# Second batch's transposed q and k in two single PSUM banks instead of the halves of a double tile, with a new order of all operations

## Chip, cores, metric

The kernel runs on one core of one Trainium2 chip. The metric is device time in microseconds (us) of one execution, as the median of several runs; lower is better.

## What is computed

Attention with a few extra "beacon" keys, and then a two-layer network with an ELU between the layers:

```
q, k, v: [B=8, H=8, S=576, D=64];  beacon_k, beacon_v: [8, 8, 16, 64]
k_all, v_all = beacon first, then k, v               # 592 keys per head
scores = q @ k_all.T / 8, causal over the 576 keys, beacons always seen
a = softmax(scores);  x = (a @ v_all) as [B*S = 4608, H*D = 512]
h = x @ w_in                                         # w_in  [512, 2048]
g = h where h > 0, else exp(h) - 1
out = g @ w_out                                      # w_out [2048, 512], float32
```

## The kernel before

Everything is cut into small steps, and the order in which they are issued is one long list of words in the code. Each engine carries out its own steps in the order of the list; semaphores, which the framework derives from the data, join the engines. A word is `step.batch.pair.part`, and a word `lv.0.1:bk` has a gate after the colon: this DMA may be issued only when the step `bk` is done. Heads are worked on in four pairs per batch.

The steps that the rest of the text names, by engine:

- POOL issues the loads. `lq.b.i.h0.h1` loads q (i = 0) or k (i = 1) of batch b for heads h0 to h1 into SBUF; only batches 0 and 1 use it. `ld` converts a quarter of a later batch's q or k into a DRAM copy. `lv`, `lb` load v, `wi` and `wo` the weights. `id` and `tri` make the identity and the triangular mask.
- SP issues `ct.b.p`: for batches 2 to 7, two DMA transposes (q and k of a pair) from the DRAM copy into the transposed tile `qk`. It also issues `s`, the stores of the output.
- PE: `T.b.p.i` transposes q or k of pair p, twelve small transposes into PSUM (batches 0 and 1). `bt` transposes the beacons' keys. `S` computes scores, `L` and `W` (batches 0) or `Y` and `Z` (later) the sums of the softmax and the products with v. `F.t.i` is a part of the first layer for token tile t, `G.t.b.q` a quarter of a 128-token block of the second. `warm.n.rows.bank.k` issues n matmuls on zeros whose results nobody reads.
- ACT: `x` is the exponential of scores, `n` and `N` the reciprocal of the sums (a logarithm, then an exponential), `e` the exponential of the ELU.
- DVE: `m` masks, `a` adds exponentials up, `M` and `V` scale the attention's output into `xT`, `r` and `g` finish the ELU, `cb` copies beacon keys into `qk`, `bs` and `bk` prepare them.
- ACT or DVE, by the last letter of the word: `cp.b.p.i` copies what T left in PSUM into `qk` (bfloat16), and `o` copies a finished block of the output out of PSUM. The last block, `os.9.3`, is copied in two halves.

Tiles of tokens: the first 512 tokens are two tiles of 256 (t = 0, 1), the others have 512 (t = 2 to 9). Batch 0 is computed in two halves of its queries (`A`, 256 queries, and `B`), so that the first tile's F can start early: `L.0.A`, `n.0.A`, `W.0.A` and `M.0.A` come ahead of it.

PSUM has eight banks here. Four of them are handed out singly by `bank()`, and T of batch 0, `bt`, `W`, `L.0.A`, `F`, `G` and the warm matmuls use them. The other four make two double tiles, handed out by `pair()`: S, L.0.B, Y and Z use them, and T of batch 1, where q and k of one pair are the two halves of one double tile. Which of the banks a step gets is written in the strings of `slots`, read one digit at each allocation. A step that gets a bank waits until the last reader of its former content is done.

Of the kernel before, what the change touches and what calls it, by code (L numbers as in the profile page):

```python
# [10 lines left out]
BF16 = mybir.dt.bfloat16  # L11
# [6 lines left out]
def kernel(  # L18
# [14 lines left out]
    B, H, S, D = q.shape  # L33
# [23 lines left out]
            "082746153804275613804275618302475613"),  # L57
        "bank": (
            "03213201320132013210213210320123010203123012021023013231023012301213210323310232"
            "30213021023023132032103212312013020213201303203213230103120310321323201321013031"  # L60
            "203102101203120312321201230130213220"),
        "qk": (
            "07651432065714320657142306574132"),
        "S": (
            "01010101010101010101010101010010101001010110010101001100101010100110011010011010"
            "010101001011001011011001101001011001101001101010101001011010"),
# [185 lines left out]
    @step  # L252
    def T(b, p, i):
        if b == 0:
            dst = tps[b, p, i] = bank(BF16, "tqk")
        else:
            if (b, p) not in tps:
                tps[b, p] = pair("tp", BF16)
            dst = tps[b, p, i] = tps[b, p][:, i, :]
        for r in range(R):  # L260
            for h in range(2):
                nc.tensor.transpose(
                    out=dst[D * h:D * (h + 1), PR * r:PR * (r + 1)],
                    in_=st[b, i][:, 2 * p + h, r, :],
                    identity=identb[0:PR, 0:PR],
                )
# [315 lines left out]
    warm.11.128.bank.0 lq.0.0.0.2 lq.0.1.0.2 lq.0.1.4.8 lq.0.0.4.8 lq.0.1.2.4 id lq.0.0.2.4 bs  # L582
    T.0.0.1 bt T.0.0.0 bk warm.4.64.bank.1 cp.0.0.0.A cp.0.0.1.V cb.0.0 lq.1.0.0.4:cp.0.0.0.A
    S.0.0.2 T.0.3.1 x.0.0.2 S.0.0.3 tri cp.0.3.1.V T.0.2.1 x.0.0.3 S.0.0.0 cp.0.2.1.V
    lq.1.1.0.4:cp.0.0.1.V T.0.3.0 x.0.0.0 S.0.0.1 lv.0.1:bk cp.0.3.0.V T.0.2.0 x.0.0.1
    warm.1.64.bank.1 cb.0.1 cp.0.2.0.V S.0.3.3 T.0.1.1 x.0.3.3 cb.0.2 S.0.2.2 cb.0.3 cp.0.1.1.V
    lb.0:cb.0.2 T.0.1.0 x.0.2.2 S.0.2.0 lv.0.2:cb.0.2 cb.1.0 warm.1.64.bank.0 cp.0.1.0.V x.0.2.0
    S.0.3.0 warm.2.64.bank.0 cb.1.1 m.0.0.3 lv.0.0:cp.0.2.0.V x.0.3.0 S.0.1.0 m.0.2.0
    warm.2.64.bank.0 wi.1.0:cb.0.0 cb.1.2 m.0.0.0 x.0.1.0 S.0.3.2 warm.2.128.bank.0 m.0.3.0 x.0.3.2
    m.0.3.3 T.1.0.1 T.1.0.0 cb.1.3 m.0.1.0 wi.1.1:m.0.3.3 cp.1.0.1.A S.0.2.3 cp.1.0.0.V L.0.A  # L590
    x.0.2.3 lv.0.4:cb.1.2 T.1.1.0 n.0.A wi.0.1:cp.0.2.0.V S.0.1.3 cp.1.1.0.V T.1.1.1
    warm.4.64.bank.0 wi.0.0:cp.1.0.0.V cp.1.1.1.V x.0.1.3 wi.2.0:cb.1.1 S.0.1.2 W.0.A.1 m.0.1.3
    wi.2.1:cp.1.0.0.V x.0.1.2 S.0.2.1 M.0.A.1 lv.0.3:m.0.0.0 W.0.A.0 x.0.2.1 m.0.0.2 S.1.0 M.0.A.0
    lq.1.1.4.8:cp.1.1.1.V x.1.0.0 S.1.2 F.0.3 lq.1.0.4.8:m.0.3.0 x.1.2.0 wi.3.0:cp.0.1.0.V S.0.1.1
    F.0.2 x.0.1.1 e.0.3 S.0.3.1 S.1.4 x.0.3.1 F.0.1 r.0.3 m.0.2.2 m.0.2.3 x.1.4.1 wi.3.1:m.0.2.2
    m.0.3.2 F.0.0 g.0.3 wo.0:m.0.2.3 e.0.2 m.0.1.2 S.1.5 e.0.0 L.0.B r.0.2 lb.1:g.0.3 m.1.2.0 e.0.1
    g.0.2 x.1.5.1 F.0.5 r.0.1 r.0.0 n.0.B g.0.0 S.1.1 lv.1.4:r.0.0 W.0.B.1.1 g.0.1 lv.1.2:g.0.0
    W.0.B.0.1 e.0.5 M.0.B.1.1 x.1.1.0 T.1.2.1 r.0.5 ld.2.0.144:g.0.1 F.0.4 M.0.B.0.1 m.1.4.1 m.1.5.1
    T.1.3.1 wo.1:m.1.4.1 cp.1.2.1.V T.1.3.0 cp.1.3.1.A T.1.2.0 g.0.5 W.0.B.0.0 cp.1.2.0.A cp.1.3.0.V
    W.0.B.1.0 m.1.1.0 S.1.3 M.0.B.0.0 S.1.9 lv.1.0:cp.1.3.0.V x.1.3.0 M.0.B.1.0 F.0.7 e.0.4 m.1.3.0  # L600
    x.1.3.1 r.0.4 F.0.6 m.1.0.0 g.0.4 e.0.7 lv.1.1:m.1.0.0 m.1.3.1 S.1.6 e.0.6 a.1.0.1 F.1.7 x.1.9.3
    r.0.7 x.1.6.2 lv.1.3:a.1.0.1 r.0.6 F.1.3 g.0.7 x.1.6.1 e.1.7 g.0.6 F.1.0 e.1.3 r.1.7 x.1.9.2
    m.1.6.1 F.1.2 r.1.3 ld.2.0.432:m.1.6.1 e.1.0 g.1.3 S.1.10 e.1.2 S.1.11 g.1.7 F.1.1 x.1.10.3
    r.1.2 wo.2:g.1.7 r.1.0 F.1.4 m.1.9.2 x.1.11.3 g.1.2 ld.2.1.288:r.1.0 S.1.7 g.1.0 S.1.8 x.1.7.2
    G.0.0.0 wo.3:g.1.2 m.1.9.3 a.1.1.1 x.1.8.2 cb.2.0 G.0.1.0 a.1.0.2 m.1.11.3 ld.2.0.0:a.1.0.2
    a.1.1.2 e.1.1 G.0.0.1 a.1.0.3 m.1.7.2 m.1.8.2 S.1.12 a.1.0.4 a.1.1.3 Z.1.0.0 x.1.12.3 m.1.10.3
    cb.2.1 r.1.1 Z.1.0.1 m.1.6.2 a.1.1.4 e.1.4 g.1.1 Y.1.0 ld.2.0.288:a.1.1.4 a.1.2.1 G.0.1.1 N.1.0
    cb.2.2 r.1.4 m.1.12.3 G.0.0.2 a.1.3.1 ld.2.1.0:m.1.12.3 F.1.5 a.1.2.2 a.1.3.2 G.0.1.2 g.1.4
    e.1.5 ld.2.1.432:a.1.3.2 a.1.3.3 G.1.0.0 a.1.2.3 a.1.3.4 r.1.5 ld.2.1.144:a.1.2.3 V.1.0.0
    G.0.0.3 g.1.5 G.1.0.1 lb.2:V.1.0.0 o.0.0.A V.1.0.2 V.1.0.1 lv.2.0:g.1.5 F.1.6 a.1.2.4 Y.1.1  # L610
    e.1.6 Z.1.1.1 r.1.6 N.1.1 cb.2.3 Z.1.1.0 g.1.6 lv.2.1:r.1.6 G.1.0.2 ct.2.0 V.1.1.1 G.0.1.3
    V.1.1.2 V.1.1.0 G.1.0.3 o.0.1.A F.2.4 o.1.0.A ct.2.1 F.2.0 e.2.4 r.2.4 F.2.2 e.2.0 g.2.4 S.2.1
    r.2.0 e.2.2 ct.2.2 S.2.2 cb.3.0 F.2.3 x.2.1.0 lv.2.2:cb.3.0 r.2.2 g.2.2 F.2.15 x.2.2.0 g.2.0
    S.2.3 e.2.15 S.2.0 ct.2.3 G.1.1.0 x.2.3.0 e.2.3 x.2.0.0 F.2.1 r.2.3 g.2.3 lv.2.3:r.2.3 G.1.1.1
    x.2.3.1 m.2.2.0 cb.3.1 s.0.1 e.2.1 m.2.0.0 r.2.15 S.2.6 lv.2.4:cb.3.1 S.2.5 m.2.3.0 g.2.15
    x.2.6.1 F.2.7 ld.3.0.0:r.2.15 x.2.5.1 m.2.1.0 a.2.0.1 F.2.10 x.2.6.2 m.2.6.1 r.2.1 e.2.7 S.2.4
    ld.3.0.144:m.2.6.1 cb.3.2 S.2.9 g.2.1 e.2.10 G.1.1.2 x.2.4.1 r.2.10 ld.3.0.288:g.2.1 F.2.8
    g.2.10 x.2.9.3 r.2.7 x.2.9.2 F.2.6 m.2.4.1 g.2.7 e.2.8 m.2.5.1 S.2.8 e.2.6 S.2.7
    ld.3.0.432:g.2.7 r.2.8 G.1.1.3 x.2.8.2 g.2.8 m.2.9.2 F.2.9 x.2.7.2 m.2.3.1 r.2.6
    ld.3.1.0:m.2.9.2 a.2.0.2 S.2.12 e.2.9 g.2.6 F.2.5 ld.3.1.144:a.2.0.2 x.2.12.3 a.2.1.1 F.2.11  # L620
    m.2.7.2 e.2.5 r.2.9 a.2.0.3 o.1.1.A S.2.10 r.2.5 S.2.11 ld.3.1.288:a.2.0.3 e.2.11 g.2.5 F.2.13
    x.2.11.3 m.2.9.3 a.2.0.4 ld.3.1.432:g.2.5 a.2.1.2 G.2.0.0 e.2.13 a.2.1.3 g.2.9 x.2.10.3 Z.2.0.0
    r.2.13 Z.2.0.1 a.2.1.4 r.2.11 Y.2.0 m.2.11.3 g.2.13 F.2.12 N.2.0 m.2.12.3 m.2.10.3 g.2.11 F.2.14
    lb.3:m.2.10.3 e.2.12 m.2.8.2 ct.3.0 a.2.3.1 G.2.3.0 e.2.14 cb.3.3 V.2.0.2 m.2.6.2 G.2.0.1 cb.4.0
    cb.4.1 V.2.0.1 lv.3.0:cb.4.1 G.2.3.1 a.2.3.2 a.2.2.1 s.0.0 G.2.0.2 ct.3.2 a.2.3.3 r.2.14
    lv.3.1:a.2.3.3 a.2.2.2 G.2.3.2 V.2.0.0 Z.2.1.1 a.2.2.3 a.2.3.4 a.2.2.4 Z.2.1.0 lv.3.2:a.2.2.3
    r.2.12 ct.3.1 g.2.14 Y.2.1 g.2.12 G.2.2.0 N.2.1 G.2.0.3 V.2.1.2 s.1.0 V.2.1.0 G.2.2.1 o.2.0.A
    lv.3.3:V.2.1.2 ct.3.3 V.2.1.1 G.2.3.3 lv.3.4:V.2.1.1 S.3.1 o.2.3.V S.3.0 x.3.1.0 F.3.0 x.3.0.0
    F.3.1 e.3.0 G.2.2.2 m.3.0.0 e.3.1 r.3.0 S.3.2 ld.4.0.0:r.3.0 G.2.2.3 x.3.2.0 S.3.6 o.2.2.V S.3.3
    x.3.6.2 F.3.10 r.3.1 x.3.3.1 g.3.1 ld.4.0.144:r.3.1 F.3.2 x.3.6.1 g.3.0 e.3.10 F.3.9 m.3.1.0  # L630
    cb.4.2 e.3.2 m.3.2.0 m.3.3.1 x.3.3.0 F.3.6 r.3.10 e.3.9 r.3.2 g.3.10 S.3.5 S.3.12 r.3.9 x.3.5.1
    F.3.5 ld.4.0.288:g.3.10 g.3.2 g.3.9 e.3.6 F.3.11 m.3.3.0 x.3.12.3 cb.4.3 r.3.6 ld.4.0.432:g.3.9
    G.2.1.0 g.3.6 e.3.5 S.3.4 r.3.5 S.3.9 a.3.0.1 F.3.4 x.3.9.3 x.3.9.2 g.3.5 G.2.1.1 m.3.6.1 e.3.4
    m.3.6.2 m.3.9.3 x.3.4.1 F.3.3 r.3.4 ld.4.1.0:m.3.9.3 g.3.4 e.3.11 S.3.8 m.3.5.1 S.3.10 e.3.3
    m.3.4.1 F.3.8 r.3.11 x.3.10.3 r.3.3 ld.4.1.144:r.3.11 g.3.11 G.2.1.2 x.3.8.2 a.3.1.1
    ld.4.1.288:g.3.11 F.3.14 m.3.9.2 e.3.8 g.3.3 ld.4.1.432:m.3.9.2 S.3.11 a.3.0.2 S.3.7 G.2.1.3
    a.3.0.3 x.3.7.2 r.3.8 g.3.8 F.3.7 o.2.1.A a.3.1.2 x.3.11.3 F.3.12 a.3.0.4 a.3.1.3 m.3.8.2
    m.3.7.2 e.3.14 m.3.11.3 Z.3.0.0 lb.4:m.3.8.2 e.3.7 a.3.1.4 r.3.14 Y.3.0 e.3.12 r.3.7 ct.4.1
    Z.3.0.1 m.3.10.3 g.3.14 N.3.0 lv.4.0:m.3.10.3 G.3.1.0 g.3.7 lv.4.1:g.3.14 r.3.12 F.3.13 a.3.2.1
    cb.5.0 V.3.0.2 G.3.2.0 s.2.1 m.3.12.3 e.3.13 lv.4.2:V.3.0.2 ct.4.0 a.3.2.2 G.3.1.1 a.3.2.3  # L640
    r.3.13 a.3.3.1 G.3.2.1 lv.4.3:r.3.13 g.3.13 G.3.1.2 a.3.3.2 s.2.2 a.3.2.4 V.3.0.1 F.3.15 ct.4.2
    a.3.3.3 G.3.2.2 lv.4.4:V.3.0.1 a.3.3.4 e.3.15 V.3.0.0 Y.3.1 r.3.15 g.3.15 Z.3.1.1 N.3.1 ct.4.3
# [111 lines left out]
```

## Time and profile before

| | |
|---|---|
| median of 6 runs | 343.56 us (342.49 to 344.72) |
| the profiled execution's own time | 343.48 us, of it a span of 341.8 us in the profile |
| PE busy (matmuls) | 333.0 us, 97% of the span |
| DVE busy | 266.1 us, 78% |
| ACT busy | 212.7 us, 62% |
| DMA | 35.82 MB in 137944 packets, 68.7% of 16 engines' span from POOL's queue |
| first transpose, first F, first F of tile 2 on PE | 6.60, 23.85, 62.55 us |

Rows of the profile read as: start, duration, engine, line of the kernel, operation, tiles out<-in, shape, count, and in brackets the idle time before it with what ended it. Rows of the waits read: who waited, for whom, us in total, times, longest. The chain that ended last is followed back from the last instruction; its shares by engine say where time went.

### The profile page before, as it was taken

How to read it: one execution, taken by the hardware profiler on the slowest of the kernel's cores; microseconds unless marked ns; L12 is line 12 of the kernel's file. 1: busy time of each engine (PE TensorE's matmuls, PEld its weight loads, DVE VectorE, ACT ScalarE, POOL GpSimd, SP SyncE). 2: the span in 40 equal slices, each digit the busy share in tenths (PEclk: the TensorE clock that was granted, in tenths of full speed). 3: DMA queues.
4: the chain of work that ended last, by engine and by line, in shares of the span. 5: the costliest groups of instructions: out<-in, count | busy, mean ns of one | idle time of the engine just before them, and what ended most of it. 6: DMA issues, size and time to landing. Idle time of an engine off the chain costs nothing.

```text
span 341.8 us, 8616 instructions
## 1 busy us (share of the span) xinstructions
PE 333.0 (97%) x3446; PEld 162.8 (48%) x3447; DVE 266.1 (78%) x739; ACT 212.7 (62%) x328; POOL 97.6 (29%) x126
## 2 busy tenths in 40 slices
PE   7989999999999999999999999999999999999995
PEld 3557755444544454444444544444444454444442
DVE  2858998589949997899569998998499859866621
ACT  2989874699268945975597649962976334634201
POOL 5685455155333452463234233021010000000000
PEclk9999999999999999999999999999999999999999
DMA  8999999999998999999989999893025000200034
GB/s 114 161 151 194 188 145 146 116 157 92 130 156 58 95 130 171 118 105 205 179 66 133 168 60 85 136 153 23 0 91 59 3 33 0 92 2 1 0 125 153
DMA packets 137944, 35.82 MB, mean 105 GB/s; under 512 B 126000, under 2 KB 133424, under 8 KB 137904
## 3 DMA queue, kind: packets, MB, share of 16 engines
q0 software_dynamic: 102240, 18.49, 68.7%
q1 hardware_dynamic: 34944, 16.52, 23.4%
q8 instruction: 27, 0.44, 0.5%
q10 hardware_dynamic: 720, 0.26, 0.3%
q14 instruction: 13, 0.11, 0.1%
HBM read 37.22 MB, written 16.52 MB: 157 GB/s over the span
## 4 chain that ended last, share of the span: by engine, by line
PE 84%; DMA 6%; DVE 4%; ACT 2%; issue 1%; POOL 1%; SPq 0%; DVEq 0%; POOLq 0%
PE ops L554 36%; PE hps L523 33%; PE sc L295 6%; PE ut L361 5%; DMA stg<-in_q_dram 2%; DMA w_in<-in_moe_w_in_dram 2%; ACT et L332 2%; DMA qk<-qkd 2%; PE lt L361 1%; DVE gt L545 1%; PE lt L465 1%; DVE r L538 1%; DVE et L348 1%; POOL w_in L204 1%; ACT e L533 1%
## 5 line engine op out<-in xcount | busy, mean ns | idle before, releaser
L523 PE MATMUL hps<-xT,w_in 128*128 128x512 f16 (+1 forms) x640 | 139.8, 358 | 0.3
L554 PE MATMUL ops<-w_out,gt 128*128 128x512 f16 x576 | 138.0, 379 | 0.0
L533 ACT ACTIVATE e<-hps 128x512 f32<-128x512 f32 x144 | 84.8, 610 | 58.6 <-PE hps L523 54.5
L332 ACT ACTIVATE et<-sc 128x1024 f16<-128x1024 f32 (+4 forms) x128 | 106.3, 877 | 20.1 <-PE sc L295 19.9
L545 DVE TENSOR_TENSOR gt<-hps,r 128x512 f16<-128x512 f32 x144 | 96.8, 686 | 2.3
L523 PEld LDWEIGHTS <-w_in 128*128 128x128 f16 x640 | 59.7, 98 | 62.4 <-issue 5.7
L538 DVE TENSOR_SCALAR r<-e 128x512 f16<-128x512 f32 x144 | 60.4, 426 | 32.6 <-ACT e L533 31.8
L554 PEld LDWEIGHTS <-gt 128*128 128x128 f16 x576 | 54.0, 98 | 65.0 <-issue 2.3
L193 POOL DMA_DIRECT2D v<-in_v_dram x40 | 33.7, 844 | 63.4 <-DVE ls L449 26.4
L348 DVE TENSOR_TENSOR et<-et,triu 128x256 f16<-128x256 f16 (+6 forms) x185 | 39.4, 253 | 7.6 <-ACT et L332 7.4
L295 PE MATMUL sc<-qk 64*128 64x80 bf16 (+19 forms) x528 | 34.8, 249 | 0.7 <-DMA qk<-qkd 0.5
L176 POOL DMA_DIRECT2D qkd<-in_q_dram x24 | 21.4, 890 | 39.0 <-DVE gt L545 13.9
L295 PEld LDWEIGHTS <-qk 64*128 64x128 bf16 x528 | 17.3, 94 | 24.9 <-issue 20.7
L449 DVE TENSOR_TENSOR ls<-ls,et 128x672 f16<-128x672 f16 (+2 forms) x84 | 28.8, 365 | 0.3
L176 POOL DMA_DIRECT2D qkd<-in_k_dram x24 | 21.3, 898 | 24.2 <-DVE et L348 4.6
L361 PEld LDWEIGHTS <-v 128*32 128x32 f16 (+1 forms) x1248 | 20.5, 96 | 9.8 <-issue 2.5
L420 DVE TENSOR_TENSOR xT<-ut,rl 128x448 f16<-128x448 f32 (+6 forms) x56 | 20.5, 415 | 4.5 <-ACT rl L495 4.5
L494 ACT ACTIVATE rl<-lt 128x576 f32<-128x576 f32 x14 | 9.1, 652 | 20.8 <-PE lt L361 20.5
L561 DVE COPY osb<-ops 128x512 f32<-128x512 f32 x17 | 11.6, 686 | 12.6 <-DMA out_dram<-osb 7.9
L561 ACT COPY osb<-ops 128x512 f32<-128x512 f32 x18 | 10.8, 599 | 15.0 <-PE ops L554 15.0
L361 PE MATMUL ut<-et,v 128*32 128x512 f16 (+4 forms) x560 | 19.3, 278 | 0.0
L449 DVE TENSOR_TENSOR ls<-et 128x928 f16<-128x928 f16 x28 | 17.7, 634 | 0.1
(49 smaller groups left out, 111.0 us busy)
## 6 DMA issues: line engine op xcount, KB each, us to landing
out_dram<-osb SPq DMA_DIRECT2D x35, 256.0 KB, 3.4
qkd<-in_q_dram POOLq DMA_DIRECT2D x24, 144.0 KB, 4.8
qkd<-in_k_dram POOLq DMA_DIRECT2D x24, 144.0 KB, 4.1
v<-in_v_dram POOLq DMA_DIRECT2D x24, 128.0 KB, 5.1
w_in<-in_moe_w_in_dram POOLq DMA_DIRECT2D x8, 256.0 KB, 7.7
w_out<-in_moe_w_out_dram POOLq DMA_DIRECT2D x4, 512.0 KB, 9.8
v<-in_v_dram POOLq DMA_DIRECT2D x8, 112.0 KB, 4.6
stg<-in_k_dram POOLq DMA_DIRECT2D x3, 288.0 KB, 6.4
```

The lines of the kernel that those rows point to most:

```text
L176: nc.gpsimd.dma_start(out=st[b, i][s0:s1], in_=(q, k)[i][b, :, s0:s1].rearrange("h s d -> s h d"))
L193: nc.gpsimd.dma_start(out=v_tile(b)[r0:r0 + n_, j, :, :], in_=v[b, :, ilo[j]:ilo[j] + n_, :].rearrange("h s d -> s h d"))
L295: nc.tensor.matmul(out=s[:, h, o0 + a - c0:o0 + e - c0], lhsT=t[D * h:D * (h + 1), 1, P * j:P * (j + 1)], rhs=t[D * h:D * (h + 1), 0, NB + ...
L332: nc.scalar.activation(out=ets[b, p][:, :, c0:c1], in_=s[:, :, o0:o0 + c1 - c0], func=AFT.Exp, bias=0.0, scale=SCALE)
L348: nc.vector.tensor_tensor(out=o, in0=o, in1=triu[0:kc[j], :, t0:t0 + e - a], op=ALU.mult)
L361: nc.tensor.matmul(out=t[32 * i:32 * (i + 1), a - qa:e - qa], lhsT=ones[0:kc[j], :] if half is None else v16[0:kc[j], j, h, half::2], rhs= ...
L449: nc.vector.tensor_tensor(out=lsum[b, p][0:kc[j], :, qj - q1:], in0=in0, in1=e_[0:kc[j], :, cj:cj + S - qj], op=ALU.add)
L523: nc.tensor.matmul(out=h[:, n_, :], lhsT=w_in16[:, cc, P * fc:P * (fc + 1)], rhs=xt[k_][:, cc, a - TT * k_:e - TT * k_], start=(cc == 0), ...
L533: nc.scalar.activation(out=eb[t, i], in_=flat(hp[t, i]), func=AFT.Exp, bias=0.0, scale=1.0)
L538: nc.vector.tensor_scalar(out=rb[t, i], in0=eb[t, i], scalar1=1.0, scalar2=1.0, op0=ALU.min, op1=ALU.subtract)
L545: nc.vector.tensor_tensor(out=flat(gt), in0=flat(hp[t, i]), in1=rb[t, i], op=ALU.max)
L554: nc.tensor.matmul(out=ob[t, tb_], lhsT=gts[t, fc][:, P * tb_:P * (tb_ + 1)], rhs=w_out16[:, fc, :], start=(fc == 0), stop=(fc == NFC - 1))
```

## The change

T of batch 1 takes a single bank for q and one for k, as in batch 0. The two double tiles are left to S, L, Y and Z. The steps themselves stay as they are; their order, the gates of the DMAs and the digits of `slots` are all new, some copies change their engine, and the warm matmuls are 24 instead of 27.

```diff
     slots = {
         "et": (
-            "082746153804275613804275618302475613"),
+            "085746123082761543028761540328716453"),
...
     def T(b, p, i):
-        if b == 0:
-            dst = tps[b, p, i] = bank(BF16, "tqk")
-        else:
-            if (b, p) not in tps:
-                tps[b, p] = pair("tp", BF16)
-            dst = tps[b, p, i] = tps[b, p][:, i, :]
+        dst = tps[b, p, i] = bank(BF16, "tqk")
...
     for word in """
-    warm.11.128.bank.0 lq.0.0.0.2 lq.0.1.0.2 lq.0.1.4.8 lq.0.0.4.8 lq.0.1.2.4 id lq.0.0.2.4 bs
-    T.0.0.1 bt T.0.0.0 bk warm.4.64.bank.1 cp.0.0.0.A cp.0.0.1.V cb.0.0 lq.1.0.0.4:cp.0.0.0.A
-    S.0.0.2 T.0.3.1 x.0.0.2 S.0.0.3 tri cp.0.3.1.V T.0.2.1 x.0.0.3 S.0.0.0 cp.0.2.1.V
-    lq.1.1.0.4:cp.0.0.1.V T.0.3.0 x.0.0.0 S.0.0.1 lv.0.1:bk cp.0.3.0.V T.0.2.0 x.0.0.1
...
-    m.0.3.3 T.1.0.1 T.1.0.0 cb.1.3 m.0.1.0 wi.1.1:m.0.3.3 cp.1.0.1.A S.0.2.3 cp.1.0.0.V L.0.A
-    x.0.2.3 lv.0.4:cb.1.2 T.1.1.0 n.0.A wi.0.1:cp.0.2.0.V S.0.1.3 cp.1.1.0.V T.1.1.1
-    warm.4.64.bank.0 wi.0.0:cp.1.0.0.V cp.1.1.1.V x.0.1.3 wi.2.0:cb.1.1 S.0.1.2 W.0.A.1 m.0.1.3
...
+    warm.9.128.bank.0 lq.0.1.0.2 lq.0.0.0.2 lq.0.1.4.8 lq.0.0.4.8 id lq.0.1.2.4 lq.0.0.2.4 T.0.0.1
+    warm.2.128.bank.1 tri bs T.0.0.0 cp.0.0.0.A bt warm.3.64.bank.1 cp.0.0.1.A bk cb.0.0
+    lq.1.1.0.4:bk cb.0.1 S.0.0.0 T.0.2.1 x.0.0.0 S.0.0.2 lq.1.0.0.4 T.0.3.1 S.0.0.3 cp.0.3.1.V
+    warm.2.128.bank.0 x.0.0.3 cp.0.2.1.V T.0.2.0 x.0.0.2 S.0.0.1 cp.0.2.0.V warm.1.128.bank.0
+    lv.0.1:cp.0.2.1.V x.0.0.1 T.0.1.1 m.0.0.0 S.0.2.2 cb.0.2 T.0.3.0 x.0.2.2 cb.0.3 m.0.0.2 S.0.2.1
+    cb.1.0 cp.0.3.0.V warm.1.64.bank.1 lv.0.0:cb.1.0 x.0.2.1 S.0.2.0 m.0.2.2 T.0.1.0 cp.0.1.1.V
+    x.0.2.0 lb.0:cb.0.0 S.0.3.0 warm.3.64.bank.2 cp.0.1.0.V lv.0.2:cb.0.1 x.0.3.0 m.0.2.0 S.0.1.0
+    wi.1.0 T.1.1.1 x.0.1.0 m.0.3.0 S.0.2.3 wi.1.1:cp.0.3.0.V T.1.0.1 x.0.2.3 S.0.3.2 m.0.1.0
+    wi.0.0:m.0.0.2 T.1.0.0 x.0.3.2 cp.1.0.0.V S.0.3.3 wi.0.1:m.0.2.2 L.0.A x.0.3.3 cb.1.1 S.0.1.3
+    lv.0.3:cb.0.3 cb.1.2 cp.1.0.1.V warm.3.128.bank.0 x.0.1.3 m.0.3.2 W.0.A.0 wi.2.1:cp.1.0.1.V
+    n.0.A S.1.2 lv.0.4:cp.0.1.0.V T.1.1.0 S.0.3.1 x.1.2.0 wi.2.0:cp.1.0.1.V W.0.A.1 M.0.A.0
+    lq.1.0.4.8 M.0.A.1 x.0.3.1 S.0.1.2 m.0.2.3 F.0.2 lq.1.1.4.8:M.0.A.1 x.0.1.2 m.0.0.3 S.0.1.1
...
+    g.0.2 e.0.0 g.0.3 S.1.0 n.0.B lv.1.1:g.0.2 W.0.B.0.1 g.0.1 W.0.B.0.0 r.0.0 x.1.0.0 F.0.4
+    M.0.B.0.0 wi.3.1:r.0.0 m.1.1.0 M.0.B.0.1 S.1.5 lv.1.4:m.1.1.0 e.0.4 S.1.4 g.0.0 W.0.B.1.1
+    x.1.4.1 cb.2.3 r.0.4 T.1.2.0 lv.1.3:cb.2.3 m.1.2.0 W.0.B.1.0 cp.1.2.0.A M.0.B.1.1 S.1.3 x.1.5.1
+    M.0.B.1.0 wo.0:cp.1.2.0.A T.1.2.1 T.1.3.1 cp.1.2.1.V F.0.5 x.1.3.1 g.0.4 cp.1.3.1.A T.1.3.0
...
+    V.1.0.0 G.0.0.2 a.1.2.3 cb.3.2 a.1.3.4 V.1.0.1 G.0.1.3 lb.2:a.1.2.3 a.1.2.4 V.1.0.2 Y.1.1 r.1.6
+    o.0.1.V Z.1.1.1 N.1.1 g.1.6 Z.1.1.0 G.1.0.3 ct.2.0 V.1.1.1 G.0.0.3 V.1.1.0 o.1.0.V F.2.15
+    V.1.1.2 o.0.0.V ct.2.1 F.2.2 e.2.15 F.2.4 e.2.2 r.2.2 F.2.0 e.2.4 g.2.2 s.0.1 S.2.0 r.2.4 e.2.0
+    S.2.2 ct.2.2 g.2.4 F.2.1 x.2.0.0 r.2.15 r.2.0 F.2.10 x.2.2.0 g.2.15 lv.2.1:r.2.0 g.2.0 S.2.1
...
```

The rest of the list goes on in the same way: the same steps, in another order, to `G.9.3.3`, `o.8.3.V` and `os.9.3` at its end (before: `G.9.3.3`, `o.9.2.V`, `os.9.3`).

## The prediction

> **What bounds the kernel now.** I read the page's header and engine table first, then the chain that ended last, the waits, and the timeline of PE, DVE and ACT in the opening.
>
> ```profile
> span 341.8 us, 8616 instructions
> ...
> PE 333.0 (97%) x3446; PEld 162.8 (48%) x3447; DVE 266.1 (78%) x739; ACT 212.7 (62%) x328; POOL 97.6 (29%) x126
> ...
> PE 84%; DMA 6%; DVE 4%; ACT 2%; issue 1%; POOL 1%; SPq 0%; DVEq 0%; POOLq 0%
> ```
>
> PE is the bound: it is busy 97% of the span and is 84% of the chain. I matched PE's records to the written steps, in order, and gave each step the shortest start-to-start time that any step of its kind took between the same neighbours (0.86 us for four 512-column matmuls of F or G). Of PE's run from 1.26 to 338.0 us, 322.1 us are then needed. 5.34 us pass before the first transpose, while DMA brings data, and 9.28 us are lost elsewhere, warm matmuls counted as lost: 0.88 before 10 us, 3.41 from 10 to 20, 1.03 from 20 to 30, 0.75 from 30 to 60, 3.2 after 60. A new order of the same work can act on these alone.
>
> The waits that the first part of the change aims at, from the waits view for PE up to 60 us, then from PE's, DVE's and ACT's timelines from 16.5 to 22 us:
>
> ```profile
> PE tp L262 <- DVE qk L281: 1.6, 3, 0.7
> ```
>
> ```profile
> 16.58 0.70 PE L262 MATMUL tp<-identb,stg 96*64 96x96 bf16 x24 [0.30 <-DMA stg<-in_k_dram]
> ...
> 18.81 0.45 PE L262 MATMUL tp<-identb,stg 96*64 96x96 bf16 x12 [0.75 <-DVE qk L281]
> ...
> 20.10 0.45 PE L262 MATMUL tp<-identb,stg 96*64 96x96 bf16 x12 [0.56 <-DVE qk L281]
> 20.48 1.03 PE L224 MATMUL w<-zero 64*128 64x512 bf16 x4
> ```
>
> ```profile
> 18.00 0.76 DVE L281 COPY qk<-tp 128x576 bf16<-128x576 bf16 x1 [0.69 <-ACT qk L281]
> ```
>
> ```profile
> 21.79 0.86 ACT L332 ACTIVATE et<-sc 128x832 f16<-128x832 f32 x1 [1.15 <-PE sc L295]
> ```
>
> Each T of batch 1 takes a half of a double tile, and the next user waits until the copies have read the whole of it: T.1.1.0 at 18.81, T.1.1.1 at 20.10, T.1.2.0 at 34.78. As the scores use the same two double tiles, S.0.1.2 comes late too, and ACT sits idle for 1.15 us at 21.79.
>
> **The change part by part.** The sum is made against the profiled execution, 343.48 us (its span of 341.8 and 1.7 around it), 0.08 below the median of 343.56.
>
> *Single banks.* These three PE waits, 1.6 us, lose their cause, and so does DVE's wait of 0.69 for ACT at 18.00. Here the page "PSUM — Partial Sum Buffer" of the Trainium skill (Terms) speaks against a cost: it forbids two engines one bank, and the halves of the double tile are two banks, so by it the 0.69 would have been zero already. The trace says that the wait is there, and the trace decides. What is late next is bank reuse, since each T now needs one of four banks that F, W and L also use: T.1.1.0 takes bank 3 after T.1.0.1's copy, T.1.2.1 bank 1 after M.0.B.1.1, T.1.3.1 and T.1.3.0 the banks of the T just before them. So 1.6 us is the most that this part gives on PE, and near zero the least. Which it is depends on the order around it.
>
> *Opening up to the first F.* Prices from the rows of before: T 0.38 us on PE, T's start to its copy 0.49, copy 0.64 on ACT and 0.75 on DVE, S 0.28, S's start to its exponential 0.40, exponentials of batch 0 0.79 apart, n.0.A 1.24, M.0.A 0.69 each. Landings: 5.75, 6.56, 9.17, 10.68, 11.39, 12.1 us for batch 0's six transfers, which leave in the same sizes, k now first. T.0.0.1 starts at 5.79 instead of 6.60, but T.0.0.0 needs the second landing: 6.6. Both copies of pair 0 are on ACT now, one after the other (before: ACT and DVE beside each other), so S.0.0.0 starts at 6.6 + 0.49 + 2 x 0.64 = 8.4 (before 8.56) and the first exponential runs 8.8 to 9.6. The next in ACT's queue belongs to S.0.0.3, behind T.0.2.1 (9.2), S.0.0.2 and T.0.3.1: 10.25 + 0.40 = 10.65; ACT is idle 1.0 us where it was idle 0.16. Four exponentials end at 13.0. The fifth needs cb.0.2, which stands on DVE behind three copies and m.0.0.0 (10.36 + 3 x 0.75 + 0.6 + 0.15 = 13.4), so it starts at 13.8, after 0.8 us idle. From there ACT runs almost without a gap (0.15): the thirteenth ends at 14.6 + 8 x 0.79 + 0.15 = 21.1, n.0.A at 22.3, both M.0.A at 23.7, and F.0.2 starts at 23.8. Before, F.0.3 started at 23.85 with the same count of PE steps done (16 S, 12 T, one L, two W). The 1.6 and 1.15 us that the banks set free are eaten by 1.6 us of new idle time on ACT. Sum to here: 0.
>
> The warm matmuls are in the rows 0.427 us apart at first and 0.216 from 7.69 on; with nine instead of eleven ahead of T.0.0.1, the two behind it cost 0.43 or 0.85. The page "TensorE: Matmul & The Clock Gate" (Part 1) says why it may be the dearer: the clock is halved until a free-running window of about 3.4 us was busy, so the change to full speed can fall late. By it T.0.0.0 could start at 7.0 and all this be 0.4 later. The rows alone bound it by 0 and 0.4; I take 0, as T.0.0.1 at 6.60 already ran at the short spacing.
>
> *Opening from the first F to the second tile.* DVE is busy without a gap over 0.25 us from 26.6 to 57.6, PE nearly so. Up to M.0.B.1.0 the rows of before give DVE 23.25 us of work, done at 37.12; the new order has 21.29 ahead of it, 10.81 of them done at 23.65. It doesn't repeat before's idle 2.81 us at 23.8: 23.65 + 10.48 + waits of 0.45 (x.0.1.2), 0.5 (n.0.B) and 0.1 = 35.2. Step by step, PE then reaches F.1.0 at 41.1 with the same ten F, eight S, four T, four W and L behind it as before at 40.96: +0.15. Up to a.1.2.4 another 22.4 us of DVE work plus 0.6 of small gaps give 58.2 (before 57.57); Y.1.1, Ln and exponential (1.35) and two V (1.5) follow, so x for the second tile is there at about 61.8, before PE wants it (62.55 then). PE keeps the lead. Three more changes between the array's forms cost 0.1 each (an F or G ahead of S takes 0.96 instead of 0.86), half of them walked already: +0.15. Sum here +0.3; bounds -1.5 (ACT's new idle is not there) and +2.
>
> *Transfers.* The weights and v stand in another order, but the POOL queue's data land one behind the other from 12 to 60 us in the trace, so only the order changes. w_in's first quarter lands at about 23, before F.0.2. ct.2.2 is 7.4 us of PE work ahead of its first score instead of 5.4; that score, S.2.6, waited: 0.865 us from 70.87 where 0.23 is needed. -0.63. On SP s.0.1 is put ahead of ct.2.2 (0.53 us at 70.40), within that lead. Batch 7's last load is 12.4 us of PE work ahead of S.7.3 (15.5 before); it needs 3.5 to land, 3.6 for three transposes issued and 2.7 to 4.2 to land, so 0, up to +1.
>
> *Steady part.* 106 changes of form instead of 105 after the first F.2: +0.1. The other losses after 60 us, 2.6 in some 25 places (F.2.8 0.31, Y.5.1 0.21), belong to the old order; a new one has its own. Bounds -1 and +3; I take +0.4, the nearest row being F.2.8's. The copies o.0.0, o.0.1, o.1.0 go from ACT to DVE (3 x 0.69) where DVE idled 1.27, 0.26 and 2.30 us, from 57.6 to 64.2: 0. The tail is the same, os.9.3 behind G.9.3.3: 0.
>
> Sum: +0.3 - 0.63 + 0.1 + 0.4 = +0.2. 343.48 + 0.2 = 343.7, with the 0.08 to the median 343.8.
>
> **The rivals.**
> Slower: DVE becomes the bound of 24 to 62 us. It takes cp.1.0.1 there (0.75) and o.0.1 ahead of g.1.6 and V.1.1.x (0.69), and each late g or M holds one of four banks that T now uses too. For it: its saturation in before. Against: the 2.81 us of idle that the new order fills. If a.1.2.4 ends after about 59 us, V.1.1.0 passes 62.55 and every microsecond more goes to the end: with both terms, the 1.6 of waits back on banks and no gain at S.2.6, 0.75 + 0.69 + 1.6 - 0.3 = +2.7, 346.3 us.
> Faster: ACT's two new idle stretches (0.84 and 0.78) do not come, because x.0.0.3 and cb.0.2 are ready earlier; then F.0.2 starts at 22.3 and the 1.6 us stay: 343.8 - 1.6 - 0.4 (a steady part no worse than before's) = 341.8. For it: the order is a different one for DMA that lands earlier. Against: landings at 9.17 and 10.68 are what this trace shows, and the DVE queue ahead of cb.0.2 doesn't depend on them.
> The double tile's wait only moves to the banks: PE's wait on copies for T stays near 1.6 us under other names, 344.8 us at most, since the walk above uses 0.4 of it. It is part of the forecast's case.
>
> **How the numbers follow.** A measurement of this kernel tells about 0.5% (1.7 us) from no change. Within that 0.42 (forecast 343.8 and the moved wait), slower 0.38 (346.3 and beyond: many new waits can add up and only 9.28 us are there to be won), faster 0.20 (341.8 and below). The range goes from 341.7, the faster case, to 347.2, the slower one plus the dearer clock (0.4) and half of the steady part's unknown; the likeliest case's own is 342.1 to 345.3.
>
> **What would show it.** Right: no PE wait of T on copies above 0.3 us before 22 us; ACT idle about 1 us before its second exponential and 0.8 before its fifth; first F at 23.8; DVE full to 58; second tile's first F at 62 to 63; S on the third pair of batch 2 without a DMA wait. Wrong: first F off by more than 1 us, PE idle in groups of F or W on DVE from 28 to 60, or over 4 us lost after 63.

## The result, and the profile after

The changed kernel takes 348.48 us (median of 35 runs, 343.30 to 352.87) where the kernel before takes 344.62 beside it (70 runs, 341.98 to 350.55). The ratio is 1.0073, with a 95% interval of 1.0048 to 1.0098: slower by some 2.5 us. (The ratio is one of means and leaves out, for each kernel, the runs more than 1.5% above its fastest, 18 of 35 and 10 of 70, so it is nearer to one than the quotient of the medians, 1.011.) On the 343.56 us of the forecast that makes 346.1: inside the range, but beyond the 1.7 us of "no change" that I held likeliest, on the side that had 0.38.

The profiled execution took 349.12 us, 5.64 more than that of before. Header, engine table and chain of its page:

```profile
span 347.4 us, 8614 instructions
PE 335.5 (97%) x3442; PEld 163.0 (47%) x3444; DVE 269.4 (78%) x744; ACT 210.9 (61%) x323; POOL 98.0 (28%) x126
PE 87%; DMA 6%; DVE 2%; issue 1%; POOL 1%; ACT 1%; SPq 0%; DVEq 0%; POOLq 0%
```

PE is still the bound. Its steps, priced as in the prediction, show where it lost time. Each column counts a step's start-to-start time beyond the shortest one of its kind:

| us lost by PE | before | after | change |
|---|---|---|---|
| start of the first T | 6.60 | 5.54 | -1.06 |
| 0 to 20 us | 4.29 | 4.93 | +0.64 |
| 20 to 60 | 1.78 | 4.32 | +2.54 |
| 60 to 200 | 2.45 | 1.42 | -1.03 |
| from 200 | 0.77 | 5.35 | +4.58 |

The changes add up to 5.67, against the 5.64 measured. The waits of PE, largest first (who waited, for whom, us in total, times, longest):

```profile
PE sc L290 <- DMA qk<-qkd: 2.8, 1, 2.8
PE w L224 <- DVE zero L131: 1.3, 1, 1.3
PE hps L518 <- DMA w_in<-in_moe_w_in_dram: 1.2, 2, 0.9
PE lt L356 <- issue: 1.1, 1, 1.1
```

The waits of T on copies (`tp L262 <- DVE qk L281`, 1.6 us before) are gone, as predicted. Three others stand in their place (the 1.3 us for `zero`, at the very start, are in before as well), and the first one alone is larger than all that was removed. PE's timeline there, late in the run, in batch 7:

```profile
236.49 1.36 PE L356 MATMUL ut<-et,v 128*32 128x512 f16 x40
237.78 1.90 PE L549 MATMUL ops<-w_out,gt 128*128 128x512 f16 x8
242.50 0.83 PE L290 MATMUL sc<-qk 64*128 64x224 bf16 x12 [2.83 <-DMA qk<-qkd]
243.27 3.31 PE L518 MATMUL hps<-xT,w_in 128*128 128x512 f16 x8
246.52 0.61 PE L290 MATMUL sc<-qk 64*128 64x64 bf16 x6
247.06 1.90 PE L549 MATMUL ops<-w_out,gt 128*128 128x512 f16 x8
```

The score that waits is S.7.12, the first one on the fourth pair of batch 7. The wait costs more than its 2.83 us: the score then takes 0.83 us, and the eight matmuls of F behind it 3.31, where eight take 1.90 in the last row. The row of the windows view (stretch, length, busy time and count of PE, weight loads, DVE, ACT, POOL; granted clock; DMA share; GB/s) shows the clock granted for these ten microseconds at 0.83:

```profile
240.00:250.00 10.00, 7.50 (x44) 2.99 (x46) 3.42 (x8) 5.17 (x8) 0.00 (x0) 0.83 0.02 3
```

Why the transposes came late is read on SP, first its timeline, then its waits from 215 to 245 us:

```profile
220.82 1.28 SPq L271 DMA_TRANSPOSE qk<-qkd  x1
229.98 1.33 SPq L562 DMA_DIRECT2D out_dram<-osb  x3
231.41 6.09 SPq L271 DMA_TRANSPOSE qk<-qkd  x4
```

```profile
SPq L562 <- ACT osb L556: 7.8, 1, 7.8
```

SP issues in the order of the list, and the new list has `s.5.2 ... s.5.1 ... s.5.3 ... ct.7.2 ... ct.7.3`. The store s.5.2 waits 7.8 us for ACT's copy o.5.2.A of a block of tile 5, and the four transposes of ct.7.2 and ct.7.3 stand behind it until 231.41. Issuing them takes to 237.5. In the profile of before the last of them are issued from 223.76 to 226.38, ahead of that store.

### The profile page after: what moved, and what is told of

Same layout as the page of the kernel before. It is cut to its first block, busy times and chain, and to the rows that moved or that the text cites. A ratio compares the mean times of both kernels' runs of the same rounds, so it can differ in the third digit from the quotient of the medians.

```text
span 347.4 us, 8614 instructions
## 1 busy us (share of the span) xinstructions
PE 335.5 (97%) x3442; PEld 163.0 (47%) x3444; DVE 269.4 (78%) x744; ACT 210.9 (61%) x323; POOL 98.0 (28%) x126
## 4 chain that ended last, share of the span: by engine, by line
PE 87%; DMA 6%; DVE 2%; issue 1%; POOL 1%; ACT 1%; SPq 0%; DVEq 0%; POOLq 0%
PE ops L549 36%; PE hps L518 35%; PE sc L290 7%; PE ut L356 4%; DMA w_in<-in_moe_w_in_dram 3%; DMA stg<-in_k_dram 2%; DMA qk<-qkd 2%; PE lt L356 2%; PE lt L460 1%; PE ub L356 1%; PE tqk L257 1%; DVE gt L540 1%; DVE qk L276 1%; ACT e L528 1%; POOL stg L165 0%
## 5 line engine op out<-in xcount | busy, mean ns | idle before, releaser
L518 PE MATMUL hps<-xT,w_in 128*128 128x512 f16 (+1 forms) x640 | 141.6, 361 | 1.3 <-DMA w_in<-in_moe_w_in_dram 1.2
L528 ACT ACTIVATE e<-hps 128x512 f32<-128x512 f32 x144 | 83.8, 606 | 61.4 <-PE hps L518 59.6
L327 ACT ACTIVATE et<-sc 128x1024 f16<-128x1024 f32 (+4 forms) x128 | 105.0, 873 | 20.4 <-PE sc L290 19.9
L290 PE MATMUL sc<-qk 64*128 64x192 bf16 (+20 forms) x528 | 34.8, 250 | 3.6 <-DMA qk<-qkd 2.8
L556 DVE COPY osb<-ops 128x512 f32<-128x512 f32 x22 | 15.1, 686 | 16.5 <-PE ops L549 16.4
L356 PEld LDWEIGHTS <-v 128*32 128x32 f16 x1248 | 20.6, 96 | 9.6 <-issue 2.9
L556 ACT COPY osb<-ops 128x512 f32<-128x512 f32 x13 | 7.6, 584 | 13.0 <-PE ops L549 13.0
```

What stands on the lines that cost most here:

```text
L290: nc.tensor.matmul(out=s[:, h, o0 + a - c0:o0 + e - c0], lhsT=t[D * h:D * (h + 1), 1, P * j:P * (j + 1)], rhs=t[D * h:D * (h + 1), 0, NB + ...
L327: nc.scalar.activation(out=ets[b, p][:, :, c0:c1], in_=s[:, :, o0:o0 + c1 - c0], func=AFT.Exp, bias=0.0, scale=SCALE)
L356: nc.tensor.matmul(out=t[32 * i:32 * (i + 1), a - qa:e - qa], lhsT=ones[0:kc[j], :] if half is None else v16[0:kc[j], j, h, half::2], rhs= ...
L518: nc.tensor.matmul(out=h[:, n_, :], lhsT=w_in16[:, cc, P * fc:P * (fc + 1)], rhs=xt[k_][:, cc, a - TT * k_:e - TT * k_], start=(cc == 0), ...
L528: nc.scalar.activation(out=eb[t, i], in_=flat(hp[t, i]), func=AFT.Exp, bias=0.0, scale=1.0)
```

## The experiments

Two theories. A: the loss is the late pair of batch 7, for which SP's order is the cause. B: it is in the opening and batch 1, up to 62 us. The two kernels for A from both sides, beside the changed kernel itself and one that takes the banks alone:

**The changed kernel once more.**

> The changed kernel as it is, timed again beside the kernels below. Both theories: 0.5 to 1.0% slower than before. Theory A (a late transpose in batch 7): its profile shows PE waiting 1 to 3 us for DMA at S.7.12, around 237 to 242 us, whatever the run. Theory B (the loss is in the opening): that wait is small in a run near the fastest, and the first F of tile 2 starts at least 1.5 us later than the 62.55 us of before.

348.70 us (12 runs), ratio 1.0089 (1.0055 to 1.0124): the slowdown is repeated, and PE again waits for `qk` at S.7.12, this time 2.54 us, with no loss on the matmuls behind:

```profile
247.41 0.61 PE L290 MATMUL sc<-qk 64*128 64x224 bf16 x12 [2.54 <-DMA qk<-qkd]
247.96 1.90 PE L518 MATMUL hps<-xT,w_in 128*128 128x512 f16 x8
```

Theory B's sign is in this profile too (352.39 us): its T take 0.69 us in the rows instead of 0.45 up to 23 us, the first F starts at 29.48 and the first F of tile 2 at 68.88, 4.6 later than in the first profile of the same kernel. So in a single run the opening can cost more than the wait.

**The two transposes early.**

```diff
-    ... Z.6.0.1 s.5.2 r.6.13 g.6.2 s.5.1 F.6.8 s.5.3 a.6.3.3 g.6.13 ct.7.2
-    G.6.3.0 ... a.6.3.4 ct.7.3
+    ... Z.6.0.1 ct.7.2 ct.7.3 s.5.2 r.6.13 g.6.2 s.5.1 F.6.8 s.5.3 a.6.3.3 g.6.13
+    G.6.3.0 ... a.6.3.4
```

> The changed kernel with one edit: ct.7.2 and ct.7.3 stand ahead of s.5.2 on SP instead of behind s.5.2, s.5.1 and s.5.3. Theory A: no DMA wait at S.7.12, 1.5 to 4.5 us faster than the changed kernel, so within 0.3% of before. Theory B: at most 0.5 us faster than the changed kernel, so 0.5% or more slower than before.

345.16 us, ratio 1.0002 (0.9977 to 1.0027), on the same chip as the run above: two words moved on SP take 3.5 us off the median (0.0087 of the ratio, 3.0 us) and 2.1 off the lowest run (345.21 to 343.16). PE's timeline at the same place:

```profile
239.34 1.90 PE L549 MATMUL ops<-w_out,gt 128*128 128x512 f16 x8
241.17 0.62 PE L290 MATMUL sc<-qk 64*128 64x224 bf16 x12
241.72 1.90 PE L518 MATMUL hps<-xT,w_in 128*128 128x512 f16 x8
```

No wait, the score at 0.62, and the F at full rate. SP issues all of batch 7's transposes by 228.3 in this run, so their data were there. By the ratio, theory A holds for nearly all of the slowdown; theory B is left with the runs whose opening goes at half rate, and with what the last group of experiments looks for.

**The same lateness in the order of before.** The store s.5.2 goes up right behind o.5.2.V, and ct.7.2 and ct.7.3 behind it.

```diff
-    ... m.6.3.0 ct.7.2 m.6.1.0 ...  S.7.3 ct.7.3 S.6.8 ...  o.5.2.V F.6.9 ...  g.7.6 s.5.2 e.7.1
+    ... m.6.3.0 m.6.1.0 ...  S.7.3 S.6.8 ...  o.5.2.V s.5.2 ct.7.2 ct.7.3 F.6.9 ...  g.7.6 e.7.1
```

> The kernel before with the reverse edit: s.5.2 is put right behind o.5.2.V, and ct.7.2 and ct.7.3 behind s.5.2. Theory A: PE waits for DMA at S.7.10, the first score of the fourth pair, for 1 to 4 us, and the kernel is 0.3 to 1.2% slower than before. Theory B: within 0.3% of before.

344.08 us, ratio 1.0003 (0.9965 to 1.0041). The wait is there, but small, and nothing of it is seen in the time:

```profile
235.22 3.63 PE L554 MATMUL ops<-w_out,gt 128*128 128x512 f16 x16
239.72 0.61 PE L295 MATMUL sc<-qk 64*128 64x448 bf16 x8 [0.88 <-DMA qk<-qkd]
240.26 1.04 PE L523 MATMUL hps<-xT,w_in 128*128 128x512 f16 x4
```

A miss in size: the order of before has two more steps of G ahead of the first score of that pair (16 matmuls in 3.63 us, where the changed kernel has 8 in 1.90). A late transpose costs only what its lead does not cover. So the next kernel also takes the lead away.

**Late, and with the lead of the changed kernel.**

```diff
 (on top of the kernel above)
-    G.6.3.2 V.6.1.1 G.6.2.2 V.6.1.0 G.6.3.3 V.6.1.2 S.7.10 S.7.4 x.7.10.3
+    G.6.3.2 S.7.10 S.7.4 V.6.1.1 G.6.2.2 V.6.1.0 G.6.3.3 V.6.1.2 x.7.10.3
```

> The kernel of before with the last two transposes of batch 7 (ct.7.2, ct.7.3) behind the store s.5.2, as in the earlier run that made them late, and S.7.10 and S.7.4 moved two G steps (3.6 us of PE work) nearer to them, so that the lead is as short as in the changed kernel. The late-transpose theory: in the earlier run the scores waited 0.9 us at 239.7; asked for at 235.2 they wait 4.5 us, two or three matmul steps behind the pause run at half rate (0.6 us more), and the median lies 3.5 to 4.5 us over the run without the shorter lead, ratio to before 1.009 to 1.013. The rival, that the loss is in the opening and the order of batch 7 costs nothing: PE makes the wait up from the steps behind it, ratio 1.000 to 1.002.

346.30 us, ratio 1.0058 (1.0028 to 1.0088), so a slowdown of this kind is made in the order of before by SP's order and the lead alone. In the median it is some half of what I expected, in part because I priced the move wrongly: the two G steps that the scores pass are 8 matmuls, 1.73 us of PE work, and not 3.6. The profiled run (348.65) shows nearly the whole:

```profile
241.13 0.61 PE L295 MATMUL sc<-qk 64*128 64x448 bf16 x8 [3.37 <-DMA qk<-qkd]
241.68 3.23 PE L554 MATMUL ops<-w_out,gt 128*128 128x512 f16 x8
244.71 1.42 PE L523 MATMUL hps<-xT,w_in 128*128 128x512 f16 x4
```

After 3.37 us of waiting, eight matmuls take 3.23 instead of 1.90 and the next four 1.42 instead of 1.03: 1.7 us more. The time differs from run to run (344.05 to 349.58); whether the wait does, one profile can't show.

**The banks alone.** Before, with T of batch 1 in single banks, the digits of `bank` and `S` given out anew and one warm group moved to bank 3; the order is unchanged.

```diff
-        if b == 0:
-            dst = tps[b, p, i] = bank(BF16, "tqk")
-        else:
-            ...
+        dst = tps[b, p, i] = bank(BF16, "tqk")
```

> The kernel before with the single banks alone: T of batch 1 takes single banks, the order stays, and the digits of the bank slots around it are assigned anew. If the single banks take PE's wait of T on copies away (1.6 us before): 0.5 to 1.6 us faster than before, first F at 22.5 to 23.4 us. If the wait moves to the banks or the time is eaten by a later bound (w_in's landing at 26.6 us): within 0.15% of before, with F.0.1 still starting at 26.6.

343.09 us (9 runs), ratio 0.9960 (0.9927 to 0.9993): by the ratio 1.4 us faster than before, with an interval that ends just short of no change. PE's waits up to 62 us:

```profile
PE tqk L257 <- DMA stg<-in_k_dram: 2.4, 3, 1.2
PE hps L518 <- DMA w_in<-in_moe_w_in_dram: 1.4, 2, 1.1
PE tqk L257 <- DVE qk L276: 0.4, 1, 0.4
```

Of the 1.6 us on copies 0.4 is left, and the first F starts at 22.70 instead of 23.85. Then F waits 1.4 us for w_in. The third F starts, before and with the banks alone, at

```profile
26.61 1.92 PE L523 MATMUL hps<-xT,w_in 128*128 128x256 f16 x16
27.07 1.92 PE L518 MATMUL hps<-xT,w_in 128*128 128x256 f16 x16 [1.06 <-DMA w_in<-in_moe_w_in_dram]
```

So both expectations came true in part, and in this profile the transfer takes all that the banks give: the first F of tile 2 is at 62.99 (62.55 before). The 0.4 us by which this profile's span is shorter come behind that, mostly from S.2.6 and F.2.8, which lost 0.64 and 0.31 us in before. Nor do the runs show that the banks make the 1.4 us. Of before's 32 runs beside it, the 10 with a recorded granted clock (the mean of the run) of 0.997 or more have a median of 343.26 us, and the other 22 one of 345.20; all nine runs of the banks alone are in the first class. At that clock the two kernels are 0.2 us apart.

**w_in earlier.** In the kernel with the banks alone, the load lv.0.4 goes behind wi.0.1 and wi.0.0.

> The kernel of before with the single banks, and the load of v's fifth piece (lv.0.4, 112 to 128 KB, about 0.7 us of the queue) behind the last two quarters of w_in that F.0.1 waits for, instead of ahead of them. If w_in's landing bounds the opening in that kernel (waits of 0.34 and 1.06 us at L518), the second wait falls to 0.3 to 0.4 us, and the time by 0.5 to 0.7 us: 342.4 to 342.6, ratio 0.994. Rival: W.0.B then waits for v, or PE gives the time back in the attention of batch 1, which waits for DVE: 343.1, ratio 0.996.

343.37 us, ratio 0.9963 (0.9932 to 0.9995), on another chip. That repeats the ratio of the banks alone, and again the runs at a clock of 0.997 or more hardly differ (343.08, 10 of 12 runs, and 343.21 before, 9 of 29). That the earlier w_in adds to it isn't shown: in the profiled run the opening is slow, the first F comes only at 26.77 and waits for no transfer.

**Warm matmuls.** The changed kernel with early transposes and eleven warm matmuls instead of nine, and the converse: the banks alone with nine instead of eleven.

```diff
-    warm.9.128.bank.0 lq.0.1.0.2 ...
+    warm.11.128.bank.0 lq.0.1.0.2 ...
```

> The changed kernel with the two transposes ahead of s.5.2, and eleven warm matmuls ahead of T.0.0.1 instead of nine. Cold-opening theory: the first T takes 0.378 us and not 0.62 (T.0.0.0 about 0.1 us earlier or equal, because the eleventh warm matmul ends at about 6.1), and the opening never stays at half rate; the run's highest time falls (346.8 with nine), the median falls by 0 to 1 us to 344.2 to 345.2. Rival, that nine or eleven is the same and the opening's half rate comes by chance of the run: median 345.2 and the same spread of 3.6 us. If the two more matmuls delay T.0.0.1 beyond its data (5.5 to 5.8), everything behind is up to 0.4 us later: 345.6.

> The kernel of before with the single banks, as in the earlier run (343.1 median, 342.3 to 344.1), but nine warm matmuls ahead of T.0.0.1 instead of eleven, as in the changed kernel. Cold-opening theory: PE idles about 1 us between the ninth and T.0.0.1 at 6.3, T.0.0.1 and in some runs all of the opening go at half rate (0.62 us for a T instead of 0.378): some of the runs 4 to 5 us longer (347 to 348), median 0 to 2 us over 343.1. Rival (nine or eleven is the same): median 343.1 and no run above 345.

With nine, the kernel with the banks takes 347.78 us (6 runs, 346.63 to 350.07; ratio 1.0113, 1.0071 to 1.0156), beside 343.37 of the run with w_in earlier on the same chip. Its profile shows half the clock from 10 to 30 us, and T at 0.69 in its rows instead of 0.45:

```profile
10.00:20.00 10.00, 10.00 (x125) 6.24 (x120) 7.90 (x29) 7.57 (x10) 4.99 (x8) 0.50 1.30 133
20.00:30.00 10.00, 10.00 (x154) 5.54 (x152) 4.32 (x10) 6.19 (x9) 6.95 (x10) 0.50 1.09 144
```

So in that order and that session nine warm matmuls cost more than 4 us, and the rival, that nine and eleven are the same, is out there. In the changed order eleven gain nothing: 347.50 (343.62 to 350.04; ratio 1.0058, 1.0021 to 1.0095), no better than the 345.16 with nine on another chip. The first T took 0.378 us as expected, but F then waited 2.29 us for w_in and ran at half rate behind it. Nor does eleven exclude the half rate: the profile of the kernel with w_in earlier, which has eleven, has a clock of 0.61 from 10 to 20 us. What decides when the clock falls in the opening, I have not settled.

**The order divided.** Four kernels ask why the changed kernel with early transposes is not as fast as the one with the banks alone. Single banks in all. The words that the order of before has up to its cut are put in the order of the changed kernel and the rest is left (twice, cut at 40 and at 62 us), the converse is made at 62 us, and the undivided order is run again.

> The order of the changed kernel (nine warm matmuls with it) up to the fourth F of tile 1, some 40 us, and from there the order of before; single banks throughout. If the new opening costs little by itself, as the step starts say (F.1.0 at 42.1 in the run with early transposes, at 41.7 in that with single banks alone), the median is 343.1 to 343.6, ratio 0.996 to 0.998. Rival: nine warm matmuls, or w_in's landing right behind them, leave PE at half rate in some of the runs; those runs are 4 us longer, the median 344.5 to 346, ratio 1.000 to 1.005.

> The order of the changed kernel up to the end of batch 1's attention (62 us), then the order of before; single banks throughout. If batch 1's stretch holds the rest of the loss (Y.1.1 idles 0.3 to 1.2 us, and tile 2 starts at 64.4 and not 63.0), the median is 1 to 1.4 us over the kernel that takes only the first 40 us: 344.2 to 345.0, ratio 1.000 to 1.002. If the loss lies behind 62 us, this kernel equals that one.

> The converse: the order of before (eleven warm matmuls) up to the end of batch 1's attention, then the order of the changed kernel with its last two transposes ahead of s.5.2; single banks throughout. If the loss that is left once the transposes are early comes from the first 62 us, this kernel is as fast as the one with single banks alone, 343.1, ratio 0.996, and none of its runs lies above 346. If it comes from the stretch behind (S.2.6's wait for a transpose, 0.5 to 1.5 us), 344.2 to 345.0, ratio 1.000 to 1.002.

> The changed kernel with the last two transposes of batch 7 ahead of s.5.2 once more, beside the three kernels that divide its order: 345.2 as in the first run (ratio 1.000), or 347.5 as with eleven warm matmuls (ratio 1.006), if that was the chip's DMA in the opening and not the warm matmuls.

| order of the changed kernel | median, us | lowest | ratio to before (95%) |
|---|---|---|---|
| nowhere (banks alone, the two runs) | 343.09, 343.37 | 342.31, 341.45 | 0.9960 (0.9927 to 0.9993), 0.9963 (0.9932 to 0.9995) |
| up to 40 us | 345.38 | 343.31 | 1.0014 (0.9978 to 1.0050) |
| up to 62 us | 345.74 | 344.35 | 1.0037 (1.0005 to 1.0070) |
| from 62 us, transposes early | 345.30 | 343.35 | 1.0011 (0.9971 to 1.0051) |
| all, transposes early (two runs) | 345.16, 344.72 | 343.16, 344.16 | 1.0002 (0.9977 to 1.0027), 1.0027 (1.0001 to 1.0054) |

One run of the kernel cut at 40 us took 1177.15 us; nothing on record says why. Every kernel with a part of the new order has a median 1.4 to 2.6 us over those with none, but among themselves their intervals overlap, only two of the five lie clear of the banks alone (up to 62 us, and the second run of all), and no part holds the loss alone. This remainder, at most 0.8% of the time, stays open. The kernel with the new order from 62 us has seven runs from 343.35 to 346.33 and five from 347.55 to 351.18, these at a recorded clock of 0.98 or less, though up to 62 us its order is that of the banks alone: so eleven warm matmuls in that order do not keep the clock up in every run. In the profile of the kernel cut at 62 us PE waits 1.3 us for DVE:

```profile
59.44 0.23 PE L460 MATMUL lt<-et,ones 128*32 128x112 f16 x4 [1.30 <-DVE xT L415]
```

That is the place of my slower rival (DVE as the bound up to 62 us), at half its price, in a divided order; in the changed kernel itself PE doesn't wait there. The version to keep is the kernel before with the single banks alone, the fastest by the ratios (0.4% under before and some 1.1% under the changed kernel), though the first of the two is not shown to come from the banks.

## Why the prediction was right or wrong

- **The number** is in the range, and that is luck. The sum came to +0.2 and the result to +2.5, most of it from a wait that neither the sum nor a rival had. The slower rival had the size (+2.7) but another cause, DVE as the bound up to 62 us, and in the changed kernel PE doesn't wait for DVE there. The range's upper end is not what its words say either: half of the steady part's +3 is 1.5, and 347.2 has 0.5 of it.
- **Batch 7's transfers** is the step that failed. The prediction took the lead of one score, S.7.3 (12.4 us of PE work after the last load, "0, up to +1"). That score didn't wait. But the fourth pair's transposes had been moved behind the store s.5.2, with 5.5 us of PE work left to S.7.12 where there were 15.5, and this was not walked. Cost in the profile: 2.83 of waiting, 0.22 on the scores and 1.41 on F behind them, 4.5 us; over many runs some 3. I had walked SP's queue for s.0.1 and ct.2.2 and not for its other stores.
- **Single banks**: right on the wait. None of T on copies above 0.3 us is left in the changed kernel, and the third rival, that it only moves to the banks, was seen for 0.4 of the 1.6 with the banks alone. What that is worth, 0 or 1.6 or between, stays open: the ratio says 1.4 us (0.2 to 2.5), the profile of the banks alone shows w_in taking all of it, and at the full clock the runs are 0.2 apart.
- **First F at 23.8**: wrong by 1.2 us, it started at 22.60. ACT idled 0.62 us ahead of its second exponential (1.0 predicted) and not at all before its fifth (0.8 predicted), nearly as the faster rival had it (22.3). Its gain didn't reach the end: F.0.1 and F.0.0 waited for w_in until 27.17, which I had called only a matter of order. They land at 25.82 and 27.12, some 0.6 later than in before (25.19 and 26.57).

```profile
22.60 1.40 PE L518 MATMUL hps<-xT,w_in 128*128 128x256 f16 x8
...
25.86 0.39 PE L518 MATMUL hps<-xT,w_in 128*128 128x256 f16 x2 [0.28 <-DMA w_in<-in_moe_w_in_dram]
27.17 1.70 PE L518 MATMUL hps<-xT,w_in 128*128 128x256 f16 x14 [0.91 <-DMA w_in<-in_moe_w_in_dram]
```

- **F.1.0 at 41.1**: 41.18. Right as a sum, with two errors in it that cancel: an earlier first F, and w_in.
- **First F of tile 2 at 62 to 63**: 64.32. DVE was near its forecast (a.1.2.4 ended at 58.97 instead of 58.2); 1.27 us are Y.1.1's, on `issue`, which no step of the sum had.
- **S.2.6**: right in that profile, no wait (-0.63). But the fourth pair of that batch, whose transposes SP issues behind those of the third, waits in other runs of the same order: S.2.11 by 0.48 us with early transposes and by 1.28 with eleven warm matmuls. The prediction priced the third pair alone, and the wait that I expected at S.2.6 with the new order from 62 us is that of S.2.11 (none came in that profile).
- **The clock**: taken at 0, where the estimate that I drew from the page "TensorE: Matmul & The Clock Gate" (Part 1) was 0.4. In the changed kernel's profile T.0.0.0 is at 7.13, nearer to the 7.0 of that estimate than to 6.6. Its second profile and that with early transposes, on one chip, have it at 7.34 and 7.20, but three profiles of the same opening on another chip at 6.39 to 6.66. So each price holds in some runs. The larger price is elsewhere: half a clock for 10 to 20 us, which the prediction did not consider. Nine warm matmuls brought it on in the order of before (+4.4 us), and the changed kernel's second profile has it.
- **Steady part**: 1.03 us less lost from 60 to 200 us, with S.2.6's 0.63 in it; the +0.4 was not needed.

## What to carry to other kernels

When an order changes, follow each in-order queue for every transfer in it: what stands ahead of it, what that waits for, and how much work lies between the transfer's landing and its first reader. A store of results waits for the end of a chain (7.8 us here), and every transfer behind it on its queue waits with it. An idle stretch of PE of some 3 us can cost half again its length, since in some runs the matmuls behind it went at half rate. And compare a gain of some 0.4% with what the clock does from run to run before you put it down to the edit.

## What the hardware showed beyond that

**Half rate after a pause.** After 2.83 and 3.37 us without matmuls, eight 512-column matmuls took 3.31 and 3.23 us instead of 1.90; after 0.88 us nothing was lost (four in 1.04). The length does not decide alone: after 2.54 us, in the changed kernel's second profile, eight took 1.90, while after 2.29 us, with eleven warm matmuls, eight of 256 columns took 1.74 instead of 1.05.

**The recorded clock can miss it.** In that second profile T takes 0.69 us from 5.76 to 23 us, as in the rows with a granted clock of 0.50, yet the clock is recorded at 1.00 throughout.

**PE waiting for nothing in the profile.** Y.1.1 stops within its 40 small matmuls, on `issue`. After, and the changed order with two more warm matmuls:

```profile
59.72 0.43 PE L356 MATMUL lt<-et,v 128*32 128x64 f16 x33
61.24 0.24 PE L356 MATMUL lt<-et,v 128*32 128x64 f16 x7 [1.09 <-issue]
```

```profile
61.27 0.41 PE L356 MATMUL lt<-et,v 128*32 128x64 f16 x31
62.84 0.26 PE L356 MATMUL lt<-et,v 128*32 128x64 f16 x9 [1.16 <-issue]
```

With two matmuls more ahead of it, the stop comes two matmuls earlier: it stands at a fixed place in PE's instruction stream, not at a piece of data. The DMA part of the page lists a queue of 27 packets of 16 KB for "instruction", one for 255 of PE's 6,886 instructions. One of these packets starts at 58.79 us in the first profile and at 60.53 in the second, 2.4 and 2.3 us ahead of PE's going on; in the run with early transposes it is 59.02 and 61.35. That PE waits there for its own code is what this fits. It was not tested by itself, the page doesn't say which engine these packets are for, and the other packets of these profiles have no such stop behind them.
